# Strassen's first product in two more batches, and second-product partial sums that stay in one PSUM bank, in a fused linear-attention and mixer kernel

## The chip, the core and the metric

The kernel runs on one core of one Trainium2 chip. The metric is the device time of one launch in microseconds.

## The reference, cut to what matters

```python
def reference(q, k, v, U, V, w_ch1, w_ch2):        # q, k, v: (8, 8, 576, 64)
    # cosine-weighted linear attention, per batch and head
    q_p, k_p = phi(q), phi(k)                      # relu(x)*cos(pos), relu(x)*sin(pos): 128 features
    kv  = einsum('bhsf,bhsd->bhfd', k_p, v)
    num = einsum('bhsf,bhfd->bhsd', q_p, kv)
    den = einsum('bhsf,bhf->bhs', q_p, k_p.sum(2))[..., None] + 1e-6
    x   = (num / den).transpose(0, 2, 1, 3).reshape(8, 576, 512)
    # mixer: a low-rank mix along the sequence, then a two-layer channel network
    u   = x + (x.transpose(0, 2, 1) @ U @ V).transpose(0, 2, 1)   # U: 576x32, V: 32x576
    return u + relu(u @ w_ch1) @ w_ch2             # w_ch1: 512x2048, w_ch2: 2048x512
```

All inputs and the output are fp32; the kernel computes the products in bf16 with fp32 sums.

## The kernel before

**Batches and tails.** Each of the 8 batches has 576 rows: four blocks of 128 (c = 0 to 3) and a tail of 64 (c = 4). The tails of two batches (a pair) are worked on together. The attention part of a batch gives x, then u, then its transpose uT; the network part is a *first product* (u @ w_ch1, with relu, into `hid`, 16 blocks of 128 hidden columns) and a *second product* (hid @ w_ch2, plus u, into the output tile `o_sb`).

**The order is written by hand.** `lay_all` (L1079) fills the list `slots`: each slot is one unit of PE work, together with the evictions that belong to it. `starts[b]` is the slot at which batch b's first product begins: 0, 32, 70, 100, 138, 168, 202 and 232 for b = 0 to 7. A first product has 16 slots (batch 7: 19), the odd batches then have 4 slots for the tails of their pair, the second product has 14 slots, and pairs 0 and 1 end with 4 slots for the second product of the tails. So the second product of batch 2 is in slots 86 to 99, of batch 4 in 154 to 167, of batch 5 in 188 to 201, of batch 6 in 218 to 231. The loop at L1427 emits slot i and then what was put beside it (`todo[i]`). Each engine runs its instructions in that order. `attention_plan(b)` (L1105) puts the attention of batch b beside slots of the batches before it.

**Attention of a batch**, in order: loads of q, k and v (SP queue, `loads`); features (`q_prep`, `k_prep`, on ScalarE and VectorE); copies of v to bf16 (`v_prep`, on GpSimd); transposes of q by DMA (`qtr_dma`, SP queue); `kv_pair`; five `x_unit`s, one for each block (8 matmuls, then three VectorE instructions); `A_unit` and `u_va` (the low-rank mix, on PE); `u_add` (VectorE, two halves: columns d = 0 and 1, and d = 2 and 3); `utr_dma`, the DMA transpose of each half of u into `uT` (SP queue, L535); `u_tail` (PE, then VectorE) and the DMA transpose of the tails.

**First product.** A plain unit (`g1_main`, L684) is four matmuls of 512 columns and a relu by ScalarE. Batches 3, 5 and 7 use Strassen's algorithm (the form with seven products and shared sums): 3 and 5 for two groups of four hidden blocks (m = 0 and 2; table `MIXED`, L797), the other eight blocks being plain, and 7 for all. In 3 and 5 the slots of a group follow `HALF` (L1023): `1`, `s4`, `6 2`, `s5`, `5 7`, `s6`, `3`, `s7 4`, where `s` units are plain ones and the digits are the seven products (`g1_part`, L610), four matmuls of 256 columns each. Products 1, 6, 5 and 3 are summed in one bank (tag T1) which ScalarE copies out after 1, 6 and 5 and reads with a relu after 3; 2 has a bank of its own (G3), 7 and 4 share one (OA). VectorE adds the copies to 2, 7 and 4 and applies relu in place. The forms of uT that Strassen needs are made by VectorE (`uT_form`, L598, four instructions `n` in the four slots before `starts[b]`). Form 0 reads columns d = 0 and 1, form 1 d = 2 and 3, forms 2 and 3 both.

**Second product** (`w_part`, L851). Batches 1 to 7 use the same algorithm: 7 products, two slots each, 8 matmuls of 256 columns a slot. The forms S1 to S4 of `hid` are made by VectorE (`hid_form`, L822), each in two halves (S3 in the place of a block of `hid`). The first halves stand beside slots 8 to 11 of the batch; in batches of `MIXED` beside 9, 11, 17 and 18 (order S1, S2, S4, S3). The second halves are emitted within the first three slots of the second product. Before the change the seven products are taken in the order 1, 6, 5, 7, 2, 3, 4 and use four banks; ScalarE copies product 1 to `w_sum`, VectorE adds product 6 to it, then `w_sum` + u goes to three quarters of the output (one by VectorE, two by GpSimd), and VectorE adds each later product into its quarter. Rows 0 to 255 of a batch are stored after slot 11 and the rest after slot 13, by the GpSimd queue for b < 6 and by the SP queue for 6 and 7.

**Banks.** PSUM tags and buffers: g (G3) 3, T (T1) 1, X (X1, two banks; X1S is the first of them) 1, oA (OA) and oB (OB) 1 each.

Of the kernel before, what the change touches and what calls it, by code (L numbers as in the profile page):

```python
# [17 lines left out]
def kernel(  # L18
# [11 lines left out]
    nc = tc.nc  # L30
# [567 lines left out]
    def uT_form(b, n):  # L598
# [204 lines left out]
    def w2_block(i, h, r=slice(0, KB)):  # L803
        return w2_h[:, r, i, h * HD : h * HD + HD]
# [13 lines left out]
    def hid_block(b, i, r, rows=slice(0, KB)):  # L818
        h = hid[b].rearrange("p (k i) t -> p k i t", i=2)
        return h[:, rows, i, r * 256 : r * 256 + 256]  # L820
# [19 lines left out]
    w_sum, w_ps, later = {}, {}, []  # L840

    def store_w(b, c, r):
        if b == 1:
# [5 lines left out]
        later.pop(0)()  # L849

    def w_part(b, n):  # L851
        step, half = divmod(n, 2)
        lhs, rhs, to = (
            (lambda: hid_block(b, 0, 0), w2_block(0, 0), 0),
            (lambda: s_forms[b, 2], T[1], 1),
            (lambda: s_forms[b, 1], T[0], 2),
            (lambda: s_forms[b, 3], T[2], 3),
            (lambda: hid_block(b, 1, 0), w2_block(1, 0), 0),
            (lambda: s_forms[b, 4], w2_block(1, 1), 2),
            (lambda: hid_block(b, 1, 1), T[3], 3),  # L860
        )[step]
        lhs = lhs()
        opens = step < 4
        if opens and half == 0:
            tag, bufs = T1 if to == 0 else G3
            w_ps[to] = bank([P, DM], FP32, tag, bufs, f"w_ps{to}")
        res = w_ps[to].rearrange("p (g n) -> p g n", g=2)
        for k_ in range(half * 4, half * 4 + 4):
            for g in range(2):
                nc.tensor.matmul(  # L870
                    out=res[:, g, :], lhsT=lhs[:, k_, g * P : g * P + P], rhs=rhs[:, k_, :],
                    start=(opens and k_ == 0 and g == 0),
                    stop=(k_ == KB - 1 and g == 1), skip_group_check=not opens,
                )
# [4 lines left out]
        lo, hi = slice(0, HD), slice(HD, DM)  # L879

        def add(eng, o, x, y):
            eng.tensor_tensor(out=o, in0=x, in1=y, op=ALU.add)  # L882

        def by_d(t):
            return t.rearrange("p c (d n) -> p d c n", n=P)

        def u(c0, h):
            return u_bf[b][:, 2 * h : 2 * h + 2, c0 : c0 + 2, :]

        if step == 0:  # L890
            w_sum[b] = pool.tile([P, 2, HD], FP32, tag="w_sum", bufs=1, name="w_sum")
            cast(A_, w_sum[b], res)
        elif step == 1:
            w = w_sum[b]
            o0, o1 = o_alloc(b, 0), o_alloc(b, 1)
            add(V_, w, w, res)
            add(V_, by_d(o1[:, :, hi]), by_d(w), u(2, 1))
            add(G_, by_d(o0[:, :, hi]), by_d(w), u(0, 1))
            add(G_, by_d(o1[:, :, lo]), by_d(w), u(2, 0))
        elif step == 2 or step == 3:  # L900
            o = o_sb[b, 1][:, :, hi]
            add(V_, o, o, res)
        elif step == 4:
            add(V_, by_d(o_sb[b, 0][:, :, lo]), u(0, 0), by_d(res))
        elif step == 5:
            o = o_sb[b, 0][:, :, hi]
            add(V_, o, o, res)
            store_w(b, 0, 0)
        else:
            o = o_sb[b, 1][:, :, lo]  # L910
            add(V_, o, o, res)
            store_w(b, 2, 1)


# [183 lines left out]

    ODDX = (5, 8, 11, 13, 15)
    QORD = (4, 0, 1, 2, 3)  # L1100

    def feature(b, f, c, i, eng):
        f(b, c, (eng, None) if i == 0 else (None, eng))

    def attention_plan(b):  # L1105
# [3 lines left out]
        def put(at, f, *a):  # L1109
            plan.append((at, lambda: f(b, *a)))  # L1110

        ops = [(f, c, i) for f in (q_prep, k_prep) for c in QORD for i in range(2)]
        if b == 2:
            for n, (f, c, i) in enumerate(ops):
                if n < 8:
                    put((25, 26, 27, 28, 28, 29, 29, 30)[n], feature, f, c, i, A_)
                elif n < 10:
                    put(24 + n, feature, f, c, i, V_)
                else:
                    put(  # L1120
                        (34, 34, 35, 36, 37, 38, 39, 39, 40, 41)[n - 10], feature, f, c, i,
                        A_ if n in (14, 17) else V_,
                    )
            V0 = 33
            at_q, at_load = (32, 34, 36), (37, 42, 43)
            kv_at, x_at, a_at, u_at = 43, (44, 46, 48, 50, 52), 54, 55
            a_bank = O1
        else:
            F, G = starts[b - 2] + (20 if odd and b < B - 1 else 16), starts[b - 1]
            late = b in (4, 6)  # L1130
            both = (0, 1, 2, 8) if late else (0, 1, 2, 10, 11, 12) if b > 3 else (1, 2, 10, 11, 12)
            for s_ in range(G - F + 2 * late):
                for eng in (A_, V_)[: 1 + (s_ in both)]:
                    if ops:
                        put(F + s_, feature, *ops.pop(0), eng)
# [23 lines left out]
            put(x_at[n], x_unit, c, *((O1, X1)[n % 2] if b < 4 else X1))  # L1159
        put(a_at, A_unit, *a_bank, A_)  # L1160
        put(u_at, u_va, (0, *X1), (2, *O1) if b < 4 else (2, OA, OB))
        d0 = 2 if odd and b - 1 in MIXED else 0
        put(u_at, u_add, d0)
        put(u_at + 2, u_add, 2 - d0)
        put(u_at + 2, utr_dma, d0, d0 + 2)
        put(u_at + 4, utr_dma, 2 - d0, 4 - d0)
        if odd:
            put(*((u_at + 1, u_tail, *T1) if b < 4 else (u_at + 3 + d0, u_tail, *X1S)))
            put(u_at + 4 + d0, utr_dma, 4, 5)
        if b < B - 1:  # L1170
            for at_, t in zip(at_load, loads(b + 1)):
                plan.append((at_, t))
# [288 lines left out]
```

## Time and profile before

| | us |
|---|---|
| three runs: median (lowest to highest) | 291.74 (291.56 to 291.79) |
| the profiled execution | 291.72 |
| its span, first to last instruction | 289.9 |
| granted TensorE clock in it | 1.000 |

Durations of single instructions, mean, from the groups of the profile:

| what | engine | ns |
|---|---|---|
| relu of a 128x512 PSUM bank (L699) | ScalarE | 597 |
| copy of a 128x512 PSUM bank (L114) | ScalarE | 596 |
| feature of q or k, 128x512 from SBUF (L305) | ScalarE | 712 |
| feature of q or k, 128x512 from SBUF (L307) | VectorE | 476 to 540 |
| add of a bank to an SBUF tile, 128x512 (L660, L882) | VectorE | 685 |
| relu in place, 128x512 bf16 (L657) | VectorE | 315 |
| S form, half, 128x1024 bf16 (L838) | VectorE | 686 |
| uT form, 128x512 bf16 (L608) | VectorE | 419 |
| add of u to a sum, 128x512 fp32 (L882) | GpSimd | 1410 |

A view of stages gives, for a stretch of the span, its length and, for each engine, busy time and number of instructions. A time-ordered view gives the start, the duration, the engine, the line, the operation and the tiles. The chain gives the start, the duration and the engine of each piece of the work that ended last. SPq is SP's queue, which issues DMAs; their landing is counted from the issue. Instructions on one engine can overlap a little: one VectorE instruction of 686 ns starts about 0.61 us after another when it doesn't read the other's result, and 0.73 us after when it does.

### The profile page before, as it was taken

How to read it: one execution, taken by the hardware profiler on the slowest of the kernel's cores; microseconds unless marked ns; L12 is line 12 of the kernel's file. 1: busy time of each engine (PE TensorE's matmuls, PEld its weight loads, DVE VectorE, ACT ScalarE, POOL GpSimd, SP SyncE). 2: the span in 40 equal slices, each digit the busy share in tenths (PEclk: the TensorE clock that was granted, in tenths of full speed). 3: DMA queues.
4: the chain of work that ended last, by engine and by line, in shares of the span. 5: the costliest groups of instructions: out<-in, count | busy, mean ns of one | idle time of the engine just before them, and what ended most of it. 6: DMA issues, size and time to landing. Idle time of an engine off the chain costs nothing.

```text
span 289.9 us, 7392 instructions
## 1 busy us (share of the span) xinstructions
PE 283.2 (98%) x3036; PEld 205.3 (71%) x3062; DVE 219.1 (76%) x447; ACT 162.1 (56%) x282; POOL 66.4 (23%) x104
## 2 busy tenths in 40 slices
PE   8999999999999999999999999999999999999995
PEld 6776455545987546876987546876888548999884
DVE  4979738886897778848895477748899587569974
ACT  2955651576593456966693456966791662067100
POOL 8430600050052303840032500341022002100210
PEclk9999999999999999999999999999999999999999
DMA  6999999999989899599949965999193303120023
GB/s 207 334 283 252 289 208 274 267 165 164 281 203 158 234 366 183 140 313 218 271 113 183 312 200 104 252 225 310 18 145 76 148 16 77 54 94 0 2 87 132
DMA packets 85447, 53.32 MB, mean 184 GB/s; under 512 B 53990, under 2 KB 83078, under 8 KB 85414
## 3 DMA queue, kind: packets, MB, share of 16 engines
q1 hardware_dynamic: 78998, 41.62, 61.6%
q0 software_dynamic: 6272, 11.17, 15.6%
q8 instruction: 24, 0.39, 0.6%
q14 instruction: 9, 0.07, 0.1%
q10 hardware_dynamic: 144, 0.07, 0.1%
HBM read 36.86 MB, written 9.44 MB: 160 GB/s over the span
## 4 chain that ended last, share of the span: by engine, by line
PE 92%; DMA 3%; DVE 2%; issue 1%; SPq 0%; DVEq 0%
PE w_ps L870 30%; PE g_ps L692 28%; PE al_ps L643 5%; PE gt_ps L723 5%; PE o_ps L763 5%; PE be_ps L643 4%; DMA vst<-in_v_dram 3%; PE x_ps L439 3%; PE kv_ps L364 3%; PE ot_ps L783 2%; PE ot_ps L971 2%; PE a_ps L465 1%; PE va_ps L495 1%; PE t_ps L382 1%; PE va_ps L518 0%
## 5 line engine op out<-in xcount | busy, mean ns | idle before, releaser
L692 PE MATMUL g_ps<-uT,w_bf 128*128 128x512 bf16 x361 | 89.5, 379 | 0.7
L699 ACT ACTIVATE hid<-g_ps 128x512 bf16<-128x512 f32 x96 | 57.0, 597 | 45.1 <-PE g_ps L692 35.5
L692 PEld LDWEIGHTS <-w_bf 128*128 128x128 bf16 x378 | 34.3, 98 | 33.6
L870 PEld LDWEIGHTS <-hid 128*128 128x128 bf16 x448 | 43.6, 98 | 5.6
L882 POOL TENSOR_TENSOR o_sb<-w_sum,u_bf 128x512 f32<-128x512 f32 x14 | 19.5, 1410 | 120.4 <-DVE w_sum L882 120.4
L870 PEld LDWEIGHTS <-S 128*128 128x128 bf16 x336 | 32.4, 98 | 4.3
L870 PE MATMUL w_ps<-T,hid 128*128 128x256 bf16 x224 | 26.9, 273 | 0.0
L870 PE MATMUL w_ps<-w_bf,hid 128*128 128x256 bf16 x224 | 26.9, 273 | 0.0
L870 PE MATMUL w_ps<-T,S 128*128 128x256 bf16 x224 | 26.3, 273 | 0.0
L882 DVE TENSOR_TENSOR o_sb<-o_sb,w_ps 128x512 f32<-128x512 f32 x28 | 19.2, 685 | 8.2 <-PE w_ps L870 7.8
L660 DVE TENSOR_TENSOR hid<-pw,be_ps 128x512 bf16<-128x512 f32 x24 | 16.5, 686 | 11.8 <-ACT pw L114 7.6
L114 ACT ACTIVATE pw<-al_ps 128x512 f32<-128x512 f32 x24 | 14.2, 596 | 18.2 <-PE al_ps L643 17.4
L506 DVE TENSOR_TENSOR u_bf<-x_bf,va_ps 128x1024 bf16<-128x1024 bf16 (+1 forms) x20 | 19.6, 1002 | 3.9 <-PE va_ps L495 3.9
L449 DVE TENSOR_TENSOR x_bf<-x_ps,rec 128x512 bf16<-128x512 f32 x28 | 19.4, 692 | 1.0
L116 POOL CAST v_ext<-vst 128x512 bf16<-128x512 f32 x24 | 17.2, 756 | 5.8 <-issue 3.7
L305 ACT ACTIVATE k_p<-kst,sinw 128x512 bf16<-128x512 f32 x26 | 17.7, 712 | 0.1
L737 POOL DMA_DIRECT2D out_dram<-o_sb x12 | 7.6, 633 | 41.1 <-DVE o_sb L771 22.8
L723 PE MATMUL gt_ps<-uT_tl,w_bf 128*128 128x128 bf16 x256 | 16.4, 219 | 0.0
L763 PE MATMUL o_ps<-w_bf,hid 128*128 128x512 bf16 x61 | 15.3, 379 | 0.2
L723 PEld LDWEIGHTS <-w_bf 128*128 128x128 bf16 x256 | 15.0, 98 | 0.4
L305 ACT ACTIVATE q_p<-qst,cosw 128x512 bf16<-128x512 f32 x21 | 14.4, 712 | 0.0
L429 DVE TENSOR_SCALAR rec<-x_ps 128x8 f32<-128x8 f32 (+1 forms) x35 | 5.7, 163 | 10.9 <-PE x_ps L439 10.5
(192 smaller groups left out, 473.0 us busy)
## 6 DMA issues: line engine op xcount, KB each, us to landing
qst<-in_q_dram SPq DMA_DIRECT2D x14, 512.0 KB, 6.2
kst<-in_k_dram SPq DMA_DIRECT2D x14, 512.0 KB, 8.3
vst<-in_v_dram SPq DMA_DIRECT2D x12, 512.0 KB, 8.7
out_dram<-o_sb POOLq DMA_DIRECT2D x12, 512.0 KB, 5.9
w_bf<-in_moe_w_ch_dram POOLq DMA_DIRECT2D x8, 512.0 KB, 10.6
out_dram<-o_sb SPq DMA_DIRECT2D x4, 512.0 KB, 3.0
qst<-in_q_dram SPq DMA_DIRECT2D x2, 640.0 KB, 5.7
kst<-in_k_dram SPq DMA_DIRECT2D x2, 640.0 KB, 13.9
```

What stands on the lines that cost most here:

```text
L116: eng.tensor_copy(out=o, in_=i)
L305: nc.scalar.activation(out=o, in_=i, func=AF.Relu, bias=0.0, scale=w)
L449: nc.vector.tensor_tensor(out=x_of(b, c, rows).rearrange("p (g i d) -> p g i d", g=2, d=D), in0=view[:, :, :, 0:D], in1=rec[rows].unsqueez ...
L506: nc.vector.tensor_tensor(out=u_bf[b][:, d0 : d0 + n], in0=x_bf[b].rearrange("p c (d n) -> p d c n", n=P)[:, d0 : d0 + n], in1=t.rearrange ...
L643: nc.tensor.matmul(out=res[:, k_, :], lhsT=lhs[:, d, k_, :], rhs=rhs[:, d, :], start=(opens and k_ == 0 and d == 0), stop=(k_ == 1 and d = ...
L660: V_.tensor_tensor(out=o, in0=x, in1=res, op=ALU.add)
L692: nc.tensor.matmul(out=g_ps.rearrange("p (c t) -> p c t", c=4), lhsT=w1_bf[:, d, j * P : j * P + P], rhs=uT[b][:, d, :, :], start=(d == 0) ...
L699: nc.scalar.activation(out=hid[b][:, j, :], in_=g_ps, func=AF.Relu, bias=0.0, scale=1.0)
L723: nc.tensor.matmul(out=g_ps[:, jj, :], lhsT=w1_bf[:, d, j * P : j * P + P], rhs=uT_tl[pr][:, d, :], start=(d == 0), stop=(d == 3),)
L763: nc.tensor.matmul(out=o, lhsT=hid[0][:, j, cc * P : cc * P + P], rhs=w2_bf[:, j, :], start=(j == 0), stop=(j == NJ - 1),)
L870: nc.tensor.matmul(out=res[:, g, :], lhsT=lhs[:, k_, g * P : g * P + P], rhs=rhs[:, k_, :], start=(opens and k_ == 0 and g == 0), stop=(k_ ...
L882: eng.tensor_tensor(out=o, in0=x, in1=y, op=ALU.add)
```

## The change

First, `MIXED` gets batches 4 and 6, so the same two groups of their first products go by Strassen's algorithm. In these two batches the relus of products 2, 7 and 4 go to ScalarE, two slots later. Second, `w_part` takes the products in another order (`W_SEQ`): product 1's bank (T1) goes on to take 6, 5 and 3, ScalarE copies the partial sum straight into a quarter of the output after 1, 6 and 5, and GpSimd adds u to three quarters in place. VectorE adds the banks of 2, 7 and 4 and takes the end of the T1 sum together with u. `w_sum` and one bank are no longer used. Third, attention is moved: for batches 5 and 7 `kv_pair` goes three slots later and the `x_unit`s five to seven, so that `u_va` is in slot 156 (it was 149) and 220 (213); the halves of u are taken with d = 2, 3 first, and transposed by DMAs put at slots 158 and 160 (were 151 and 153), and 222 and 224 (215 and 217); `u_tail` is in 164 (152) and 225 (216). The transposes of q for batches 4 and 6 go one or two slots later, and the v copies of batch 3 eight slots earlier. The slots of `uT_form` are as before: 164 to 167 for batch 5, 226 to 229 for batch 7; batches 4 and 6 get theirs, at 134 to 137 and 198 to 201.

```diff
+    RELU_A = (4, 6,)
+    relus = []
+
+    def late_relus():
+        for r in list(relus):
+            r[0] -= 1
+            if r[0] < 1:
+                relus.remove(r)
+                r[1]()
...
         def relu(o):
+            if b in RELU_A:
+                relus.append([
+                    2,
+                    lambda: nc.scalar.activation(
+                        out=o, in_=o, func=AF.Relu, bias=0.0, scale=1.0
+                    ),
+                ])
+                return
             V_.tensor_scalar(out=o, in0=o, scalar1=0.0, scalar2=None, op0=ALU.max)
...
-    MIXED = {3: (0, 2), 5: (0, 2)}
+    MIXED = {3: (0, 2), 4: (0, 2), 5: (0, 2), 6: (0, 2)}
+    FULL = [b for b, ms in MIXED.items() if 2 in ms]
...
+    W_SEQ = (
+        (1, 0), (1, 1), (2, 0), (6, 0), (6, 1), (2, 1), (7, 0),
+        (5, 0), (5, 1), (7, 1), (3, 0), (3, 1), (4, 0), (4, 1),
+    )
...
     def w_part(b, n):
-        step, half = divmod(n, 2)
...
+        p, half = W_SEQ[n]
+        lhs, rhs, to = {
+            1: (lambda: hid_block(b, 0, 0), w2_block(0, 0), 0),
+            2: (lambda: hid_block(b, 1, 0), w2_block(1, 0), 1),
+            3: (lambda: s_forms[b, 4], w2_block(1, 1), 0),
+            4: (lambda: hid_block(b, 1, 1), T[3], 2),
+            5: (lambda: s_forms[b, 1], T[0], 0),
+            6: (lambda: s_forms[b, 2], T[1], 0),
+            7: (lambda: s_forms[b, 3], T[2], 2),
+        }[p]
         lhs = lhs()
-        opens = step < 4
+        opens = p in (1, 2, 7)
         if opens and half == 0:
-            tag, bufs = T1 if to == 0 else G3
-            w_ps[to] = bank([P, DM], FP32, tag, bufs, f"w_ps{to}")
+            w_ps[to] = bank([P, DM], FP32, *(G3 if to else T1), f"w_ps{to}")
...
-        if step == 0:
-            w_sum[b] = pool.tile([P, 2, HD], FP32, tag="w_sum", bufs=1, name="w_sum")
-            cast(A_, w_sum[b], res)
-        elif step == 1:
-            w = w_sum[b]
-            o0, o1 = o_alloc(b, 0), o_alloc(b, 1)
-            add(V_, w, w, res)
-            add(V_, by_d(o1[:, :, hi]), by_d(w), u(2, 1))
-            add(G_, by_d(o0[:, :, hi]), by_d(w), u(0, 1))
-            add(G_, by_d(o1[:, :, lo]), by_d(w), u(2, 0))
-        elif step == 2 or step == 3:
-            o = o_sb[b, 1][:, :, hi]
-            add(V_, o, o, res)
-        elif step == 4:
-            add(V_, by_d(o_sb[b, 0][:, :, lo]), u(0, 0), by_d(res))
...
+        def add_u(r, h):
+            add(G_, by_d(o(r, h)), by_d(o(r, h)), u(r, h))
+
+        if p == 1:
+            cast(A_, o(0, 0), res)
+            add_u(0, 0)
+        elif p == 6:
+            cast(A_, o(1, 0), res)
+            add_u(1, 0)
+        elif p == 5:
+            cast(A_, o(1, 1), res)
+        elif p == 2:
+            add(V_, o(0, 0), o(0, 0), res)
+        elif p == 7:
+            add(V_, o(1, 1), o(1, 1), res)
+            add_u(1, 1)
+        elif p == 3:
+            add(V_, by_d(o(0, 1)), u(0, 1), by_d(res))
             store_w(b, 0, 0)
         else:
-            o = o_sb[b, 1][:, :, lo]
-            add(V_, o, o, res)
+            add(V_, o(1, 0), o(1, 0), res)
             store_w(b, 2, 1)
...
+    X5 = (5, 8, 10, 12, 14)
...
-            V0 = starts[b - 2] + 9 if b > 3 else F + 9
-            at_q, at_load = (F + 5, F + 7, F + 7), (F + 8, F + (16 if late else 14), V0 + (8 if late else 5))
+            V0 = starts[b - 2] + 9 if b > 3 else F + 1
+            at_q, at_load = (F + 7, F + 8, F + 8) if late else (F + 5, F + 7, F + 7), (F + 8, F + (16 if late else 14), V0 + (8 if late else 5))
             if b == 3:
                 at_q = (F + 6, F + 7, F + 8)
-                at_load = (F + 11, F + 14, V0 + 5)
+                at_load = (F + 11, F + 14, F + 14)
...
+            elif b - 1 in FULL:
+                kv_at, x_at = G + 1, [G + i for i in ODDX]
             elif b - 1 in MIXED:
-                kv_at, x_at = G + 1, [G + i for i in ODDX]
+                kv_at, x_at = G + 1, [G + i for i in X5]
...
-        d0 = 2 if odd and b - 1 in MIXED else 0
+        d0 = 2 if odd and b - 1 in FULL else 0
...
         if odd:
-            put(*((u_at + 1, u_tail, *T1) if b < 4 else (u_at + 3 + d0, u_tail, *X1S)))
-            put(u_at + 4 + d0, utr_dma, 4, 5)
+            late_t = 3 if b == 5 and b - 1 in FULL else 0 if b - 1 in FULL else 1 if b - 1 in MIXED else 0
+            put(*((u_at + 1, u_tail, *T1) if b < 4 else (u_at + 3 + d0 + late_t, u_tail, *X1S)))
+            put(u_at + 4 + d0 + late_t, utr_dma, 4, 5)
...
     for i, s in enumerate(slots):
+        late_relus()
         s()
```

More of the change, by code (lines that the diff above doesn't have):

```diff
@@ L838, in hid_form @@
         V_.tensor_tensor(out=o, in0=a, in1=b_, op=op)
-    w_sum, w_ps, later = {}, {}, []
+    w_ps, later = {}, []
+    W_SEQ = (
+        (1, 0), (1, 1), (2, 0), (6, 0), (6, 1), (2, 1), (7, 0),
+        (5, 0), (5, 1), (7, 1), (3, 0), (3, 1), (4, 0), (4, 1),
+    )
     def store_w(b, c, r):
@@ L851, in w_part @@
     def w_part(b, n):
-        step, half = divmod(n, 2)
[L853 to L861, printed above, removed]
+        p, half = W_SEQ[n]
[8 more added lines that the diff above has]
+        }[p]
         lhs = lhs()
-        opens = step < 4
+        opens = p in (1, 2, 7)
         if opens and half == 0:
-            tag, bufs = T1 if to == 0 else G3
-            w_ps[to] = bank([P, DM], FP32, tag, bufs, f"w_ps{to}")
+            w_ps[to] = bank([P, DM], FP32, *(G3 if to else T1), f"w_ps{to}")
         res = w_ps[to].rearrange("p (g n) -> p g n", g=2)
@@ L878, in w_part, with u, o, add @@
             return
[L879 to L882 removed]
         def by_d(t):
             return t.rearrange("p c (d n) -> p d c n", n=P)
[L887 to L907 removed]
+        def u(r, h):
+            return u_bf[b][:, 2 * h : 2 * h + 2, 2 * r : 2 * r + 2, :]
+        def o(r, h):
+            return o_alloc(b, r)[:, :, h * HD : h * HD + HD]
+        def add(eng, o_, x, y):
+            eng.tensor_tensor(out=o_, in0=x, in1=y, op=ALU.add)
+        def add_u(r, h):
[15 more added lines that the diff above has]
+            add(V_, by_d(o(0, 1)), u(0, 1), by_d(res))
             store_w(b, 0, 0)
         else:
[L910 to L911 removed]
+            add(V_, o(1, 0), o(1, 0), res)
             store_w(b, 2, 1)
```

## The prediction

> **What bounds the kernel.** I read the page first, then what PE waited for, then stages, then the chain and the time-ordered views inside them.
>
> ```profile
> PE 283.2 (98%) x3036; PEld 205.3 (71%) x3062; DVE 219.1 (76%) x447; ACT 162.1 (56%) x282; POOL 66.4 (23%) x104
> PEclk9999999999999999999999999999999999999999
> PE 92%; DMA 3%; DVE 2%; issue 1%; SPq 0%; DVEq 0%
> ```
>
> ```profile
> PE w_ps L202 <- DVE zero L125: 1.2, 1, 1.2
> PE t_ps L394 <- POOL v_four L116: 0.2, 1, 0.2
> PE xz L1186 <- DVE k_p L307: 0.2, 1, 0.2
> ```
>
> The second view is complete: PE waited three times, all in the warm-up, and never in a product. So the time is the sum of PE's work: work taken from PE counts in full, work on DVE, ACT, POOL or SP counts only from where it makes PE wait. The stages (length, busy time and count of PE, PEld, DVE, ACT, POOL, then clock, DMA share, GB/s), first product of batch 4, second of 4, first of 5, second of 6:
>
> ```profile
> 161.41:177.91 16.50, 16.39 (x148) 8.13 (x149) 11.59 (x24) 9.13 (x16) 3.93 (x7) 1.00 0.68 198
> 177.91:190.13 12.22, 12.22 (x114) 10.95 (x113) 9.32 (x17) 9.76 (x16) 3.42 (x3) 1.00 0.98 197
> 190.13:205.13 15.00, 14.84 (x153) 10.60 (x154) 10.17 (x23) 10.53 (x19) 3.54 (x6) 1.00 0.85 251
> 240.10:252.33 12.23, 12.23 (x114) 10.96 (x113) 8.15 (x14) 1.19 (x2) 2.77 (x2) 1.00 0.16 31
> ```
>
> No stage has slack on PE, while DVE is already at 76% of the even second product. From the chain, the price of the two kinds of first product:
>
> ```profile
> 162.53 1.73 PE g_ps L692 x8
> 190.13 0.44 PE al_ps L643 x4
> 177.91 12.23 PE w_ps L870 x112
> ```
>
> A plain 512-column matmul costs 1.73/8 = 0.2163 us, a 256-column one 12.23/112 = 0.1092.
>
> **Saving.** In batches 4 and 6 each half (m = 0, 2) turns 16 wide matmuls into 28 narrow ones: 16 x 0.2163 - 28 x 0.1092 = 3.46 - 3.06 = 0.40. Four halves: **-1.60 us**. The second product keeps its 112 matmuls, so PE's work there is unchanged.
>
> **Edits that I cost at nothing, and their cover.** The second product loses three DVE adds a batch (0.61 to 0.69 each), gains two ACT copies (0.60) and one POOL add (1.41). DVE and POOL time alone is not on the path. The ACT copies are: bank T1 now carries product 1, then 6, 5 and 3 on top, so PE may add 6 only when ACT has read 1. Before it stands unit (2,0), 8 x 0.109 = 0.87 us; the copy took 0.60 and began 0.08 after PE's end (second product of 4: 179.66 to 179.74). Products 5 and 6 have one and two units of cover; of 5 it is again 0.87, and the ACT features ahead of that copy are four, 4 x 0.61 = 2.44 of the 3.5 us since the copy before. Cover gone, each copy would cost its 0.6, 21 copies 12.6 us; but L643 already runs part 1, s4 (0.86), part 6 on one bank with no gap, so I take 0, at most 0.1 a batch. In the first products of 4 and 6 ACT does 16 evictions (0.50 apart) and 6 relus: their price lies between 0.597 (from PSUM) and 0.712 (from SBUF); SBUF is their source, so I take 0.71. 8.0 + 6 x 0.71 + key-value copy 0.6 = 12.9 us of some 15.7: covered. DVE there: six adds 4.1, five x units of 1.04, two forms 1.4: 10.7, covered. Batch 3's v copies, eight slots earlier, stand ahead of POOL's add for product 6 of batch 1 and wait for v's load; that add is read only by product 4's, seven units (6 us) later. The q transposes of batches 4 and 6 move one or two slots back, and on SP those of 6 now stand behind both u transposes of batch 5, from 10.3 us after the second product of 4 begins. SP took 4.5 to 9.4 us to issue a q pair and some 2.6 for q's loads; behind them stands u_tail's transpose, so it goes out at 18 to 24 and lands 2.5 to 6.9 later; the first tail unit wants it at 14.1 + 15.0 = 29.1. With the row of that batch (7.1) it lands at 25: 0, worst case 2. X5 and the 1 in late_t are never reached.
>
> **Where a wait is made.** Batch 5's and 7's attention moves five to seven slots later, into the second products of 4 and 6, so the transposes of u (SP) land just ahead of the forms that read them (uT_form, L608), whose slots have not moved. DVE runs in order: a form that waits for its DMA holds up the next eviction. Rows for the transposes:
>
> ```profile
> 148.76 1.24 SPq L535 DMA_TRANSPOSE uT<-u_bf  x1
> 147.51 1.21 DVE L506 TENSOR_TENSOR u_bf<-x_bf,va_ps 128x1024 bf16<-128x1024 bf16 x1
> DMA to landing us min/median/max: 3.3/3.3/3.3
> 216.16 1.28 DVE L506 TENSOR_TENSOR u_bf<-x_bf,va_ps 128x512 bf16<-128x512 bf16 x2
> ```
>
> SP issues 0.04 us after the add ends; landing, from the issue, was 3.2 to 3.3 in three windows, at DMA shares of 0.26 to 0.81, 3.5 to 4.5 behind q's transposes, 4.8 and 6.0 with loads under way, 2.5 for the small tail. Bounds 2.5 and 6.0; I take 3.3, since no load or q transpose stands ahead of these two on SP.
>
> *Second product of 6* (clock zero at its first matmul). PE: a unit is 0.874; A (0.39), va (0.37) and u_tail (0.34) come in between, so unit 12, product 4 on the bank of product 7, is due at 12 x 0.874 + 1.10 = 11.59. DVE: the last x unit ends 1.60; six S forms (0.61 apart, 0.73 where one reads the one before) 1.60 + 2 x 0.73 + 4 x 0.61 = 5.50; u_add of d 2-3 (two pieces, 1.19) 6.69; u_add of d 0-1 (1.21) 7.90. SP issues 7.94, lands 11.24. uT_form 0 reads d 0-1 and stands at slot 226 ahead of the add of product 7 (slot 227): it starts 11.3, the add 11.65 to 12.34, PE goes on at 12.4. **+0.82.** Range: landing 2.5 gives 0.02, 4.5 gives 2.0.
>
> *Second product of 4.* DVE has batch 6's features at three early slots too (0.40 each). The last S3 form starts 1.60 + 0.73 + 4 x 0.61 + 2 x 0.40 = 5.57 and ends 6.3; PE wants S3 at unit 6, 6 x 0.874 + 0.76 = 6.0. Before, these half forms of even batches stood in slots 10 and 11 of the first product. **+0.30** (0 to 0.6). Then the u_adds end at 6.18 + 1.19 + 0.40 + 1.21 = 8.98, the DMA lands 12.3; form 0 starts 12.4 (slot 164, after product 7's add), u_tail's add 12.75, product 3's add, which frees T1, 13.36 to 14.05. Batch 5's first part needs T1 at 14 x 0.874 + 1.10 + 0.30 = 13.64: **+0.43** (0 to 3.1).
>
> *Second product of 2.* POOL's new add of u, ahead of DVE's add of product 2, stands behind batch 4's v copies:
>
> ```profile
> 114.31 5.03 POOL L116 CAST v_ext<-vst 128x512 bf16<-128x512 f32 x4 [2.04 <-DMA vst<-in_v_dram]
> 128.74 2.29 POOL L116 CAST v_ext<-vst 128x512 bf16<-128x512 f32 x4 [1.86 <-issue]
> ```
>
> They end 119.3, the POOL add 120.6, DVE's add of 2 at 121.3, a feature, its add of 7 at 122.4; PE wants that bank at 112.26 + 12 x 0.874 = 122.75. Margin 0.3, and four copies took 5.03 here against 2.29 elsewhere: I take **+0.10** (0 to 1.6).
>
> The Trainium skill (SBUF — State Buffer, Who interferes with whom) says that a DVE instruction with two SBUF inputs and a GpSimd instruction that reads SBUF exclude each other, the second waiting for the whole of the first. The two rows above fit it. It speaks against this change, which puts POOL's adds among DVE's S forms; what that would do is the last rival.
>
> **Sum.** 291.72 (span 289.9 and 1.8 around it) - 1.60 + 0.82 + 0.30 + 0.43 + 0.10 = 291.77; the profiled run stands 0.02 under the median, so **291.8 us**. This case's own range, stalls of 0.9 to 2.4: 291.0 to 292.5.
>
> **Rivals.** *No stall*: DVE reaches the u_adds some 0.9 us sooner than my chain (fewer waits between x units and forms), or the DMAs land at 2.5; then 291.74 - 1.60 = 290.1. For it: DVE loses three adds a batch, and forms and features are its only work there. Against: the chain uses only measured spacings and none of the three adds stood ahead of these u_adds. *Late landing* (slower): the d 0-1 transpose of batch 5 or 7 lands later than 3.3 us. Past that, all of it goes to PE, in each of the two stages, since DVE stands at form 0; it decides from about 0.3 us in both (291.8 + 0.6). At 4.5 in the second product of 4 alone: 293.0; in both: 294.2. For it: the share of DMA there was 0.98; against: loads of batch 7 now stand before or behind, not beside. *POOL locked out* (slower): POOL's add in the second product of 2 is stretched as the worst v copy was, 2.90 against 0.61, so 2.3 us; DVE's add of 2 waits, then of 7, PE waits 2.3 - 0.3 - 0.4 = 1.6: 291.8 + 1.5 = 293.3. Against: DVE's S forms there are over by 116.3, before this add can start.
>
> **Chances.** Forecast 0.50, no stall 0.30, late landing 0.12, POOL 0.08. About 0.2% (0.58 us) is what can be told from no change: 291.16 to 292.32. Of the forecast's 0.50, 0.34 lie inside, 0.10 below, 0.06 above: faster 0.40, same 0.34, slower 0.26. The range reaches to the no-stall case and over the single late landing: 290.1 to 293.2; beyond it lie both landings late, some of the POOL case, and a saving above 1.60.
>
> **What will show it.** First products of 4 and 6 shorter by 0.8 each but for moved pieces; 64 wide matmuls fewer on the plain line (L692), 112 more on the Strassen line (L643). PE waits of 0.3 at product 7 of batch 4, 0.4 at batch 5's first part (by DVE's add on T1) and 0.8 at product 4 of batch 6, with DVE idle before uT_form on a DMA of uT. No such idle time: the no-stall case. PE waits on ACT in the second products would make the sum wrong from a side that I cost at nothing.

## The result, and the profile after

The changed kernel takes **294.33 us** (median of 4 runs, 293.66 to 295.36) against 291.76 (291.56 to 291.82) on the same chip: a ratio of 1.0091, 95% interval 1.0076 to 1.0106. It is 2.57 us slower, and outside the range that was predicted. Its profiled execution took 294.1 us with a span of 292.3. Four runs of two kernels below took 296.8 to 298.4 us, far above the other runs of the same kernel; ratios leave them out, and where a median holds them the one without them is given beside it.

From the page of the kernel after: busy time of each engine, the granted clock in 40 slices, and the chain's share by engine.

```profile
PE 284.5 (97%) x3110; PEld 210.6 (72%) x3110; DVE 221.7 (76%) x446; ACT 175.6 (60%) x308; POOL 74.1 (25%) x111
PEclk9999999999999999999999999999999999999999
PE 90%; DVE 6%; DMA 2%; issue 1%; DVEq 0%
```

PE fell from 92% of the chain to 90% and DVE rose from 2% to 6%. What PE waited for, the whole view of the kernel after (engine, line, awaited instruction: total, times, longest):

```profile
PE al_ps L653 <- DVE o_sb L912: 1.3, 2, 0.9
PE w_ps L202 <- DVE zero L125: 1.2, 1, 1.2
PE w_ps L892 <- DVE hid L857: 0.8, 1, 0.8
PE w_ps L892 <- DVE o_sb L912: 0.5, 1, 0.5
PE va_ps L518 <- DVE u_bf L506: 0.4, 1, 0.4
```

Before, no wait stood inside a product; now four rows, 3.0 us, do, and each names VectorE. The stages of the kernel after, bounded by PE's first matmul of each: first and second product of batch 4, second of 5, first and second of 6 (columns as before: length, then busy time and count of PE, PEld, DVE, ACT, POOL):

```profile
160.08:175.60 15.52, 15.52 (x169) 11.11 (x168) 9.81 (x22) 11.90 (x23) 3.93 (x7) 1.00 1.12 297
175.60:190.77 15.17, 13.95 (x161) 11.40 (x159) 13.06 (x23) 11.20 (x20) 4.37 (x3) 1.00 0.41 70
...
209.90:224.13 14.23, 13.34 (x152) 11.32 (x149) 14.08 (x27) 10.18 (x18) 4.09 (x3) 1.00 0.78 121
224.13:239.65 15.52, 15.52 (x169) 11.11 (x169) 11.01 (x26) 11.91 (x22) 1.26 (x2) 1.00 0.17 70
239.65:254.61 14.96, 14.01 (x161) 11.39 (x158) 12.49 (x20) 2.69 (x6) 3.76 (x3) 1.00 0.23 45
```

The first products of 4 and 6 run without a gap. In the second products PE is idle for about one us each, and VectorE is busy for 13.06 of 15.17, 14.08 of 14.23 and 12.49 of 14.96 us. The lengths that these three have without a wait were measured later, in a kernel without PE waits there (the kernel with the sums of W1 late, below): 13.61, 13.17 and 13.62. So the stalls are 1.56, 1.06 and 1.34, together **3.96 us**.

The saving follows from the same cuts. 13.61 is 1.38 more than the second product of 4 before (12.23): that much attention moved into it. From batch 3's first tail matmul of the output to the second product of 4 it was 21.16 us before (156.58 to 177.74) and is 18.97 (156.63 to 175.60): 21.16 - 1.38 - 18.97 = **0.81**. For batch 6, from the second product of 5 to that of 6: 30.88 (209.06 to 239.94) - 1.38 - (29.75 - 1.06) = **0.81**. Both were predicted at 0.80. The balance is -1.62 + 3.96 = +2.34, and the two profiled spans differ by 2.4.

Where VectorE lost its time is seen in single instructions. The time-ordered view of DVE in the second product of 4 of the kernel after:

```profile
178.51 1.38 DVE L307 TENSOR_SCALAR q_tl<-qst,sinw 64x512 bf16<-64x512 f32 x1
179.81 1.28 DVE L857 TENSOR_TENSOR S<-hid,S 128x1024 bf16<-128x1024 bf16 x2
181.02 0.47 DVE L307 TENSOR_SCALAR q_p<-qst,sinw 128x512 bf16<-128x512 f32 x1
...
189.10 0.43 DVE L608 TENSOR_TENSOR tb<-uT 128x512 bf16<-128x512 bf16 x1 [1.90 <-DMA uT<-u_bf]
...
190.04 0.68 DVE L912 TENSOR_TENSOR o_sb<-u_bf,w_ps 128x512 f32<-128x512 bf16 x1
```

and GpSimd's in the same kernel, three of its nine adds in these stages:

```profile
178.28 1.33 POOL L912 TENSOR_TENSOR o_sb<-o_sb,u_bf 128x512 f32<-128x512 f32 x1 [13.08 <-ACT o_sb L114]
...
220.91 1.61 POOL L912 TENSOR_TENSOR o_sb<-o_sb,u_bf 128x512 f32<-128x512 f32 x1 [3.61 <-DVE o_sb L912]
...
242.33 1.33 POOL L912 TENSOR_TENSOR o_sb<-o_sb,u_bf 128x512 f32<-128x512 f32 x1 [15.12 <-ACT o_sb L114]
```

The feature at 178.51 took 1.38 us for 64x512, while the same form on 128x512 took 0.47 at 181.02. It starts 0.23 us after a GpSimd add, and that add ends at 179.61; the feature ends 0.28 later. So it did its work only when the add was over. The other two adds do the same to DVE, in the second products of 5 and 6:

```profile
221.52 1.29 DVE L608 TENSOR_TENSOR tb<-uT 128x512 bf16<-128x512 bf16 x1
...
242.75 2.06 DVE L857 TENSOR_TENSOR S<-hid,S 128x1024 bf16<-128x1024 bf16 x2
...
245.93 2.40 DVE L506 TENSOR_TENSOR u_bf<-x_bf,va_ps 128x512 bf16<-128x512 bf16 x3
```

A uT form of 0.43 took 1.29, a pair of S forms of 1.28 took 2.06. The adds of u at 245.93 ran at their usual pace, though a GpSimd add began at 245.88: their second input is a PSUM bank. This is the lock that the Trainium skill (SBUF — State Buffer, Who interferes with whom) describes: it names VectorE instructions with two SBUF inputs, and features of this kind when they run in a mode with two ports, and says that whichever issues first holds the shared pair for its whole length. The trace agrees in the lengths: the held feature and the held uT form end 0.28 and 0.29 us after the add, and the adds of u keep their time. In which mode a feature ran, no view shows. That GpSimd can be the one that is held shows in its add at 181.83, which began beside S forms already under way and took 1.88 us.

### The profile page after: what moved, and what is told of

It reads as the page before. It is cut to its first block, busy times and chain, and to the rows that moved or that the text cites. A ratio compares the mean times of both kernels' runs of the same rounds, so it can differ in the third digit from the quotient of the medians.

```text
span 292.3 us, 7551 instructions
## 1 busy us (share of the span) xinstructions
PE 284.5 (97%) x3110; PEld 210.6 (72%) x3110; DVE 221.7 (76%) x446; ACT 175.6 (60%) x308; POOL 74.1 (25%) x111
## 4 chain that ended last, share of the span: by engine, by line
PE 90%; DVE 6%; DMA 2%; issue 1%; DVEq 0%
PE g_ps L710 23%; PE w_ps L892 23%; PE al_ps L653 7%; PE be_ps L653 5%; PE gt_ps L741 5%; PE o_ps L781 5%; PE w_ps L202 3%; PE x_ps L439 3%; PE kv_ps L364 2%; PE ot_ps L801 2%; DMA uT<-u_bf 2%; PE ot_ps L994 2%; DVE u_bf L506 1%; DVE o_sb L912 1%; PE a_ps L465 1%; PE va_ps L495 1%
## 5 line engine op out<-in xcount | busy, mean ns | idle before, releaser
L710 PE MATMUL g_ps<-uT,w_bf 128*128 128x512 bf16 x314 | 77.0, 379 | 0.0
L717 ACT ACTIVATE hid<-g_ps 128x512 bf16<-128x512 f32 x80 | 47.4, 597 | 31.8 <-PE g_ps L710 26.6
L912 POOL TENSOR_TENSOR o_sb<-o_sb,u_bf 128x512 f32<-128x512 f32 x21 | 28.4, 1352 | 126.8 <-ACT o_sb L114 105.4
L710 PEld LDWEIGHTS <-w_bf 128*128 128x128 bf16 x314 | 29.1, 98 | 25.9
L678 DVE TENSOR_TENSOR hid<-pw,be_ps 128x512 bf16<-128x512 f32 x36 | 24.7, 687 | 20.7 <-ACT pw L114 10.7
L114 ACT ACTIVATE pw<-al_ps 128x512 f32<-128x512 f32 x36 | 21.3, 595 | 18.7 <-PE al_ps L653 10.1
L114 ACT ACTIVATE o_sb<-w_ps 128x512 f32<-128x512 f32 x21 | 12.5, 597 | 22.1 <-PE w_ps L892 15.7
L912 DVE TENSOR_TENSOR o_sb<-o_sb,w_ps 128x512 f32<-128x512 f32 x21 | 14.3, 680 | 8.5 <-POOL o_sb L912 3.3
L653 PEld LDWEIGHTS <-sa 128*128 128x128 bf16 x192 | 17.7, 98 | 4.0 <-issue 0.2
L653 PEld LDWEIGHTS <-w_bf 128*128 128x128 bf16 x144 | 14.0, 98 | 5.2 <-issue 1.7
L116 POOL CAST v_ext<-vst 128x512 bf16<-128x512 f32 x24 | 16.0, 705 | 6.0 <-DMA vst<-in_v_dram 3.0
```

The costliest lines, as they stand in the source:

```text
L114: nc.scalar.activation(out=o, in_=i, func=AF.Copy, bias=0.0, scale=1.0)
L653: nc.tensor.matmul(out=res[:, k_, :], lhsT=lhs[:, d, k_, :], rhs=rhs[:, d, :], start=(opens and k_ == 0 and d == 0), stop=(k_ == 1 and d = ...
L678: V_.tensor_tensor(out=o, in0=x, in1=res, op=ALU.add)
L710: nc.tensor.matmul(out=g_ps.rearrange("p (c t) -> p c t", c=4), lhsT=w1_bf[:, d, j * P : j * P + P], rhs=uT[b][:, d, :, :], start=(d == 0) ...
L717: nc.scalar.activation(out=hid[b][:, j, :], in_=g_ps, func=AF.Relu, bias=0.0, scale=1.0)
L912: eng.tensor_tensor(out=o_, in0=x, in1=y, op=ALU.add)
```

## The experiments

Theory A: GpSimd's new adds of u shut VectorE out; VectorE is then late for the transposes of u and for the S and uT forms that PE needs. Theory B: the work that moved into the second products (attention, forms that wait for a landing) makes the stalls, and would without the adds.

**The two halves alone.** The second product alone:

```diff
-    MIXED = {3: (0, 2), 4: (0, 2), 5: (0, 2), 6: (0, 2)}
-    FULL = [b for b, ms in MIXED.items() if 2 in ms]
+    MIXED = {3: (0, 2), 5: (0, 2)}
+    FULL = []
```

> The second half of the change alone: the table of batches is 3 and 5 again, so batches 4 and 6 have plain first products and the attention of 5 and 7 stands where it was; the new order of the second product, ScalarE's copies and GpSimd's adds stay. Theory A (GpSimd's new adds hold VectorE up by 0.8 to 0.9 us each, and what VectorE does late holds a bank that PE wants): the lock is there, but VectorE has time left before PE wants a bank, so no wait of PE over 0.2 and 291.7 us (291.4 to 292.3). Theory B (only the late transposes of u cost): 291.7. If ScalarE's copies or the order of the second product cost PE time by themselves, it is over 292.5.

Measured 291.95 us (10 runs, ratio 1.0006, 0.9984 to 1.0027), and no PE wait in a product, as both theories had it. The new second product costs nothing where the attention stands as before. The lock is there all the same: in the second product of 6 an S form took 1.64 us (at 242.94), and in that of 4 two GpSimd adds took 4.09 (at 180.52) while the S forms and features beside them, the first of them already under way, kept their 0.68 and 0.47. But VectorE had time left. The first product alone: `w_part` as it was, and `V0` of batch 3 back at F + 9.

> The first half alone: batches 4 and 6 by Strassen with the moved attention and forms, and the second product as before the change (its order, four banks, w_sum, GpSimd's two adds after product 6; batch 3's copies of v where they were). Saving 1.6. Theory A: GpSimd's adds come only after product 6, when VectorE's S forms are over, and the last banks are freed earlier; what stays is S3 late in batch 4 (0.3), and u_tail of batch 7, whose bank is held until VectorE's u_add, now behind two more adds (about 1.4): 292.0 (291.0 to 293.0). Theory B: the transposes go out later than in the changed kernel, since VectorE's adds into w_sum stand ahead of u_add, so it is not faster than the changed kernel: 294 or more.

Measured 292.85 (ratio 1.0031, 1.0008 to 1.0053): inside the range of A. Its second product of 5 took 13.18 us, without a stall; those of 4 and 6 took 14.82 and 14.90. So batches 4 and 6 stall with the old second product too: 1.12 of the 2.57 us come with the first product alone. No VectorE form or feature is stretched in these two stages (a pair of S forms took 1.28 or 1.29 us), so these stalls are not the lock: PE waited 1.0 us for a VectorE add in the one, and 1.2 for the add of u that frees `u_tail`'s bank in the other.

**Without GpSimd's adds.**

```diff
         def add_u(r, h):
-            add(G_, by_d(o(r, h)), by_d(o(r, h)), u(r, h))
+            return
```

> The changed kernel without GpSimd's adds of u in the second products of batches 1 to 7 (three quarters of those outputs lack u); all else stays. Theory A: no VectorE form or feature in the second products of 4, 5 and 6 takes 1.3 us or more, the waits of PE fall from about 4.4 to about 1.7 (the recorded 0.8, 0.3 and 0.4), so 291.7 us (291.2 to 292.3). Theory B: the transposes are as late as before, 293.5 or more.

Measured 292.28 (ratio 1.0017, 0.9993 to 1.0040). No form or feature is stretched. PE's waits in products, from the view of this kernel:

```profile
PE al_ps L653 <- DVE o_sb L912: 1.0, 1, 1.0
PE w_ps L892 <- DVE o_sb L912: 0.6, 1, 0.6
```

The wait on an S form (0.8) and that on u's add (0.4) are gone, and the second product of 5 is down from 14.23 to 13.33. The other two stand at 14.85 and 14.36: 1.24 and 0.74 are left. So the lock makes 3.96 - 0.16 - 1.24 - 0.74 = 1.82 us of the stalls, and 2.14 have another cause, most of it as predicted: VectorE's add that frees the bank stands behind a uT form that waits for its DMA. The form in the second product of 4 of this kernel:

```profile
188.63 0.42 DVE L608 TENSOR_TENSOR tb<-uT 128x512 bf16<-128x512 bf16 x1 [2.48 <-DMA uT<-u_bf]
```

Without the lock the prediction's chain fits: the adds of u ended 8.91 us after the start of the second product of 4 (8.98 predicted) and 7.93 after that of 6 (7.90), and PE went on with product 4 of batch 6 at 12.61 (12.4). Only in the second product of 4 is there something else: SyncE took 2.29 us to issue the first transpose of u, so the second one, which form 0 reads, went out 0.89 us after its add, and form 0 began at 13.17 for 12.4.

**The forms behind that add.**

```diff
-            put(starts[b] - 4 + n, lambda b=b, n=n: uT_form(b, n))
+            put(starts[b] - (2 - n // 2 if b == 5 else 4 - n), lambda b=b, n=n: uT_form(b, n))
-        put(s6 + 24 + n, lambda n=n: uT_form(B - 1, n))
+        put(s6 + 28 + n // 2, lambda n=n: uT_form(B - 1, n))
```

> The changed kernel with the forms of uT for batches 5 and 7 emitted behind VectorE's add of product 3 (slots 166, 166, 167, 167 and 230, 230, 231, 231 in place of 164 to 167 and 226 to 229), so that a form that waits for its DMA holds up no eviction. If it is VectorE's order that makes PE wait: the wait for T1 in front of batch 5 (0.57 with its restart) and for product 4 of batch 6 (0.64) go, S3's and u_tail's and those of the second product of 5 stay: 293.1 (292.8 to 293.4). If it is the landing itself (first products want the forms as soon as they land): 294.0 or more.

Measured 293.04 (ratio 1.0062, 1.0030 to 1.0094). The waits of the second products of 4 and 6 on that bank are gone (lengths 14.59 and 14.34); the wait on the S form, that on u's add and the one in the second product of 5 stand. Each cause alone gives back a part.

**Moves that keep every computation.** If A holds, placing GpSimd's adds where VectorE reads PSUM should do what leaving them out did.

```diff
             cast(A_, o(0, 0), res)
-            add_u(0, 0)
...
             cast(A_, o(1, 0), res)
-            add_u(1, 0)
...
             add(V_, o(0, 0), o(0, 0), res)
+            add_u(0, 0)
+            add_u(1, 0)
```

With these adds behind VectorE's add of product 2, and all uT forms of 5, 6 and 7 behind product 3's add:

> The changed kernel with two edits: GpSimd's adds into the first two quarters are emitted behind VectorE's add of product 2, so they run beside adds that read PSUM and not beside S forms; and the forms of uT for batches 5, 6 and 7 stand behind the add of product 3. Theory A (lock, and order on VectorE): the waits of T1 and of product 4 go in all three second products, S3 of batch 4 stays (0.3, with the restart of PE up to 0.5): 290.6 us (290.3 to 291.2). Theory B (landing itself): 292.5 or more.

Measured 293.0 (10 runs, 291.96 to 298.11; without the two longest 292.35; ratio 1.0034, 1.0004 to 1.0065): a miss. Its profile is of the longest of these runs, so its trace is not compared. With the S4 and S3 half forms of batches 4 and 6 in the first products besides:

```diff
-(9, 11, 17, 18)[i] if b in MIXED else 8 + i
+((9, 11, 12, 14) if b in RELU_A else (9, 11, 17, 18))[i] if b in MIXED else 8 + i
```

> As the run before, and the first halves of S4 and S3 of batches 4 and 6 beside slots 12 and 14 of the first product, in place of 17 and 18. Theory A: no wait of PE is left, so the whole saving of 1.6 is seen: 290.2 us (289.9 to 290.6). If more work of VectorE in the first product holds a bank there, PE waits in the first products of 4 and 6 and it is 291 or more.

Measured 292.54 (10 runs, ratio 1.0025, 1.0016 to 1.0034): faster than the change, not as expected. The second products of 4 and 6 are free of waits (13.61 and 13.62), but that of 5 has grown. From the stage and time-ordered views of this kernel:

```profile
208.79:223.71 14.92, 13.50 (x152) 11.33 (x150) 14.78 (x26) 10.18 (x18) 3.89 (x3) 1.00 0.75 115
```

```profile
216.35 1.78 DVE L307 TENSOR_SCALAR k_p<-kst,cosw 128x512 bf16<-128x512 f32 x2
...
218.05 1.71 DVE L591 TENSOR_TENSOR sa<-w_bf 128x512 bf16<-128x512 bf16 x2
...
216.52 2.62 POOL L912 TENSOR_TENSOR o_sb<-o_sb,u_bf 128x512 f32<-128x512 f32 x2 [20.13 <-DVE o_sb L912]
```

VectorE was busy for 14.78 of 14.92 us. The adds had moved from beside the S forms to beside batch 7's k features and the sums of W1 for batch 7 (`w1_form`, 0.75 a pair alone, 1.71 here). The lock had a new victim, on the same path. Two of the moves were also run alone. The adds alone behind product 2:

> The changed kernel with GpSimd's adds behind the add of product 2 and nothing else; no work is left out. Theory A: as the run without these adds (292.3), or a little over it where an add now runs beside a form of uT: 292.4 (292.1 to 292.9). If it is the amount of GpSimd's work and not its neighbours on VectorE, it stays at 293.7 or more.

Measured 294.13 (ratio 1.0082, 1.0063 to 1.0100): by its time this is the rival's case. But the wait on the S form went, and the second product of 5 rose from 14.23 to 15.26: there two pairs of W1 sums took 1.71 us each beside adds (at 218.40 and 221.03), and a pair without one 0.75 (223.00). The neighbours had changed; that it is they and not the amount of work is settled below, by a kernel with the same adds and these sums elsewhere. The S forms alone:

> The changed kernel with the first halves of S4 and S3 of batches 4 and 6 in slots 12 and 14 of the first product and nothing else; GpSimd's adds and the forms of uT stay as in the changed kernel. It frees VectorE of 1.2 us ahead of u_add in the second products of 4 and 6. If VectorE's queue is what makes the transposes late and PE wait: the waits for S3, T1, u_tail and product 4 go there (3.0 in all), the 1.06 of the second product of 5 stays: 291.3 (290.9 to 292.0). If the lock by GpSimd alone decides, its 0.8 a stage stays and it is 292.8 or more.

Measured 293.75 (ratio 1.0068, 1.0042 to 1.0094). This is not the 291.3 of the first case. The second product of 6 gained 0.93, that of 4 only 0.23: the S form was in time, but SyncE took 2.48 us to issue the first of the two transposes of u (1.25 in the kernel after), and the wait moved on to bank T1 (1.2 us).

**VectorE emptied beside the adds.** Six of the eight sums of W1 move from the second product of 5 into the first of 6, the other two behind the adds:

```diff
-            put(s6 - 6 + n, lambda n=n, m=m: w1_form(n, m + 1))
+            put(s6 + (-3, 1, 2, 3)[n], lambda n=n, m=m: w1_form(n, m + 1))
```

> The second product of batch 5 took 14.92 us in the kernel with all three moves, where 13.0 is its length without a wait, and VectorE was busy for 14.78 of it: two pairs of the sums of W1 for batch 7 took 1.71 us a pair beside a GpSimd add, a pair 0.75 alone. Here six of these eight sums move into the first product of batch 6, in whose first five us VectorE is idle for 2.7 us, and the other two behind the GpSimd adds. Lock theory (VectorE is late there because GpSimd's adds shut it out): the second product of 5 comes down to 13.0-13.3 us, nothing is lost in the first of 6 (15.8), and the time is 290.8 us (290.2 to 291.4), below the kernel before. Rival (the product waits for k features, landings or the banks themselves): 292.2 or more, with a wait of over 1 us left in the second product of 5.

Measured **290.78** (12 runs, 290.58 to 292.96; before 291.87 in 29 runs; ratio 0.9968, 0.9952 to 0.9984), as expected and below the kernel before. The whole view of PE's waits in this kernel:

```profile
PE w_ps L202 <- DVE zero L125: 1.2, 1, 1.2
PE xz L1213 <- ACT k_p L305: 0.4, 1, 0.4
PE t_ps L394 <- ACT q_p L305: 0.4, 1, 0.4
PE o_ps L781 <- DMA w_bf<-in_moe_w_ch_dram: 0.3, 1, 0.3
```

None is left in a product of batches 2 to 7. From its six stages, first product of 4 to second of 6:

```profile
160.60:176.37 15.77, 15.60 (x168) 11.02 (x169) 10.65 (x23) 12.14 (x23) 3.92 (x7) 1.00 1.03 292
176.37:189.98 13.61, 13.61 (x161) 11.47 (x158) 11.65 (x22) 11.00 (x19) 3.85 (x4) 1.00 0.47 70
...
209.12:222.29 13.17, 13.17 (x151) 11.31 (x149) 12.63 (x22) 10.18 (x18) 4.08 (x4) 1.00 0.85 131
...
238.05:251.67 13.62, 13.62 (x163) 11.47 (x159) 10.17 (x18) 2.59 (x5) 3.42 (x3) 1.00 0.25 49
```

VectorE's busy time in the second products is down by 1.41, 1.45 and 2.32 us against the kernel after, through the forms that moved and the lock that went. It has not gone everywhere: three of batch 7's k features still took 3.07 us beside two adds of GpSimd, from the time-ordered view of this kernel:

```profile
216.68 3.07 DVE L307 TENSOR_SCALAR k_p<-kst,cosw 128x512 bf16<-128x512 f32 x3
...
220.75 0.69 DVE L912 TENSOR_TENSOR o_sb<-u_bf,w_ps 128x512 f32<-128x512 bf16 x1 [0.40 <-PE w_ps L892]
```

But now VectorE waits for PE at 220.75, not the other way round. Two more kernels ask what is left. The tail of u of batch 5 issued ahead of the q transposes on SyncE (`late_t` 0):

> As the kernel with the sums of W1 late, and the tail of u of batch 5 made three places earlier, so that its transpose goes out on SyncE ahead of the q transposes and q loads and not behind them. Where both kernels have their u tail in time, the same time within 0.2 us and less spread; if the tail's transpose still lands too late in some executions, this one is faster by up to 1 us in the median. Against it: the transpose waits on SyncE for the add of u's tail, and the q transposes behind it go out later; then a wait in the second product of 5 and 0.3 us more.

Measured 290.86 (12 runs, 290.56 to 292.86; ratio 0.9970, 0.9957 to 0.9984): the same time with the same spread. In its profiled execution the second product of 5 took 13.62 us, with a wait of 0.4 for ScalarE. The place of that transpose is not what spreads these times. And that kernel with the sums of W1 late, its GpSimd adds left out:

> The kernel with the sums of W1 late and GpSimd's three adds of u left out of each second product (u is then missing from three quarters of the outputs of batches 1 to 7). Nothing shuts VectorE out. If the moves have taken every VectorE instruction that counts away from the GpSimd adds, within 0.3 us of that kernel (290.5 us). If a lock is left on the path, it is faster by that much, down to 290.0; if it is slower or above 291.5, something other than the adds holds the second products.

Measured 290.88 (ratio 0.9960, 0.9944 to 0.9976), with second products of 13.61, 13.17 and 13.61 us: to 0.01 those with the adds. In the change the same omission was worth 1.8 us of the stalls, here nothing that the runs can tell (290.88 against 290.78): the adds cost only through what VectorE does beside them.

**The last gap.** The two first products of that kernel are 0.25 longer than the change's (15.77 and 15.76 for 15.52). In the view of waits PE's weight loads for an x unit wait twice, 0.7 us in all, for VectorE's x_bf, which an S form precedes. So the S forms went back to where the change has them:

> The kernel with the sums of W1 late, without the move of the S4 and S3 half forms (they go back to the change's places in the second products of 4 and 6). In the kernel with that move the last x unit of each of these first products started 0.24 us late, since its weight load waited for VectorE's x_bf, behind an S form; there is no PE wait left elsewhere. Lock theory: with GpSimd's adds gone from beside them the S forms run at 0.69 us and S3 is in time within 0.1 us where they stand, the two gaps of 0.24 go, and u's transposes start two forms (1.2 us) later, for which the forms have 1 us of slack in the second product of 4 and more in that of 6: 290.4 us (290.2 to 290.9). Rival: the two forms more ahead of the adds of u make uT land too late again: a wait of 0.5 us or more at T1 or at product 4's bank in each, 291.3 or more.

Measured 290.79 (12 runs; without the two of 298.4 it is 290.70, and the others lie from 290.00 to 294.14; ratio 0.9960, 0.9932 to 0.9988). In its profiled execution (290.69, span 288.9) the gaps are gone, PE waits only in the warm-up, and the second products take 13.68, 13.18 and 13.62. By the stages it is 0.40 better than the kernel with the S forms early; the medians, 290.70 and 290.78, don't tell the two apart.

The stages and the time side by side. "Stretch" runs from batch 3's first tail matmul of the output to the end of the second product of 6:

| kernel | second of 4 | of 5 | of 6 | stretch against before (95.58) | median against before |
|---|---|---|---|---|---|
| the change | 15.17 | 14.23 | 14.96 | +2.40 | +2.57 |
| first product alone | 14.82 | 13.18 | 14.90 | +0.94 | +1.12 |
| no GpSimd adds | 14.85 | 13.33 | 14.36 | +0.58 | +0.55 |
| forms behind the add | 14.59 | 14.24 | 14.34 | +1.22 | +1.31 |
| adds behind product 2 | 14.68 | 15.26 | 14.43 | +2.41 | +2.31 |
| S forms early | 14.94 | 14.23 | 14.03 | +1.74 | +1.93 |
| these three moves | 13.61 | 14.92 | 13.62 | +0.69 | +0.72 |
| and sums of W1 late | 13.61 | 13.17 | 13.62 | -1.06 | -1.09 |
| the same, tail of u early | 13.61 | 13.62 | 13.62 | -0.61 | -1.01 |
| and sums of W1 late, no adds | 13.61 | 13.17 | 13.61 | -1.06 | -0.99 |
| and sums of W1 late, S forms back | 13.68 | 13.18 | 13.62 | -1.46 | -1.31 |

The stretch, read from one profiled execution of each kernel, follows the median within 0.2 us, but for the kernel with the tail of u early (0.40), whose profiled execution took 1.0 us more than its median. Outside the stretch the spans of the profiled executions differ by up to 0.9 us from that before. So these stages account for the medians, not for every single execution.

## Why the prediction was wrong

**The saving, -1.60: right.** 0.81 and 0.81 were measured, from 0.80 and 0.80.

**"DVE and POOL time alone is not on the path", costed at nothing: the step that failed.** GpSimd's time is not on the path, but its adds take VectorE's time, and VectorE's order is the path here. Put as durations the adds were rightly sized (1.35 in the mean, where 1.41 was read); what was missing is that VectorE instructions stand still beside them. Leaving them out took 1.82 of the 3.96 us of stalls away. The sum had 1.65 us of stalls, and without the adds 2.14 were measured: so the lock is most of what the sum lacked. The rule was at hand, and the prediction quoted it as a rival; it applied it only to the second product of 2, with GpSimd as the one that waits. That stage came out at 12.25 against 12.23 before, where +0.10 was taken; the lock struck the other engine, in three other stages.

**Second product of 6, +0.82: measured 1.34.** The mechanism was the one described, mis-sized in the chain ahead of it. The adds of u were to start 5.50 us after the stage began, behind the S forms, and started at 6.28 (245.93): the pair of S forms that took 2.06 for 1.28 explains the 0.78. They ended 0.78 late as well (8.68 for 7.90), the transpose landed from its issue in 3.22 where 3.3 was taken, form 0 began at 251.80 and product 4 at 252.87, 13.22 after the stage's start for 12.4. On PE's side the moved attention costs 1.38, not 1.10, so product 4 was due 0.28 later than the prediction had it. Between them stands the wait for bank X (0.4), which the prediction did not see: `u_tail` needs that bank, and the late add of u frees it.

**Second product of 4, +0.30 and +0.43: measured 1.56.** S3 ended 7.09 us after the start where 6.3 was taken, and the 0.91 that the feature lost covers that: PE waited 0.80 where 0.30 was taken; without the adds it did not wait there. The adds of u ended at 185.42, 9.82 after the start and not 8.98, again by the lock; the landing took 3.63 where 3.3 was taken. With the 0.41 that PE waited for T1, the view of waits names 1.21 of the 1.56; the other 0.35 it puts down to nothing.

**Second product of 5, costed at nothing: measured 1.06.** It had no term. The lock stretched an S form (213.32, 1.53 us) and, just ahead of product 3's add on T1, a uT form (1.29 for 0.43); PE waited 0.89 for that add.

**Costed at nothing, rightly:** ScalarE's copies (no PE wait on ScalarE in a second product), its relus, the u tail behind q on SyncE, and, of the third move, batch 3's v copies (no PE wait in the second product of 1).

**The rivals.** "No stall" at 290.1 is what the change would be worth in another order: 290.7 to 290.9 was reached, 1.0 to 1.3 below before, with 1.46 in the traced stretch. "Late landing" had the right place, since DVE stands at form 0 for 1.90 and 2.26 us in the two stages, but the landings took 3.63 and 3.22 us, so only one was past the 3.3 taken, by 0.33; the adds of u were 0.84 and 0.78 late. The GpSimd case had the right mechanism in the wrong place and direction. What the runs don't separate is how much of the 2.14 us left without the adds belongs to late issue and landing and how much to the order of the forms. In the last kernel, with the adds, the forms of uT and the sums of W1 moved, both are gone. A landing of 4.6 us in the kernel with the sums of W1 late cost nothing in the second product of 4.

## What to carry to other kernels

Work on an engine that is far from its limit is not free if it shuts out one that is near its own: ask which VectorE instructions stand beside each GpSimd instruction, and charge each that reads two SBUF tiles, or makes a feature from fp32, with the rest of the GpSimd instruction's length (0.8 to 0.9 us here). Moving such an instruction moves the lock to its new neighbours, so look at those first; a place beside VectorE's reads of PSUM cost nothing here. When the sum of a tuned kernel comes out near zero, the stalls were sized on spacings from the kernel before, and any stretch ahead of an in-order wait adds to all that follow.

## What the runs showed that was not expected

- Beside a GpSimd add of 1.16 to 1.61 us (128x512, fp32, from SBUF), single VectorE instructions took 1.29 for 0.43 (uT form), 1.53 for 0.69 (S form) and 1.38 for 0.47 (feature, fp32 to bf16); instructions with one PSUM input kept their time (an add of 0.69 at 220.75 in the kernel with the sums of W1 late, the adds of u 2.40 for three).
- In these stages of the change the engine that lost was mostly VectorE, since GpSimd's add had issued first. The reverse shows in an add of 1.88 us at 181.83 and in one of 1.61 at 220.91, which began while S forms and W1 sums were under way, and in the second product alone (two adds in 4.09).
- SyncE took 1.23 to 2.48 us to issue one transpose of u in these stages, and the landings ranged from 3.0 to 5.0 us from the issue.
- Attention between the products costs more than its matmuls: 1.38 us where their durations, less their overlap, gave 1.10.
